# Copying half of a masked weight into natural rows from SyncE's queue instead of ScalarE's, around the last weight piece

## The chip, the core and the metric

The kernel runs on one core of a Trainium2 chip. The metric is device time in microseconds (us) of one execution, taken as the median of several runs. TensorE is written PE in the profile, VectorE DVE, ScalarE ACT, GpSimd POOL and SyncE SP. A name with a q (SPq, ACTq) is the engine's own queue of instructions, from which transfers (DMAs) are issued.

## What is computed

A weight `w` of 1024 x 1024 is pruned: in each group of four consecutive rows k, column by column, the two entries of largest magnitude are kept and the others set to zero. Then 8192 tokens `x` (16 x 512) are multiplied by it and a bias is added. All inputs and the output are bf16.

```python
wg = w.reshape(G, M, D)                       # G = 256, M = 4
mag = jnp.abs(wg)
order = jnp.argsort(mag, 1)
thr = jnp.take_along_axis(mag, order[:, M - N:M - N + 1, :], 1)   # N = 2
mask = mag >= thr
wp = (wg * mask).reshape(D, D)
return jnp.einsum("bsd,df->bsf", x, wp) + b
```

## The kernel before

**The data.** Tokens are worked on in 64 tiles of 128. The 1024 output columns are two halves of 512 (h = 0, 1), one PSUM bank each; there are eight banks, taken in turn. The contraction over k is eight blocks of 128 rows, and the first four (g = 0) and last four (g = 1) are handled apart at the start.

**The weight.** It is loaded into four tiles `w_gh[(g, h)]` of 128 partitions x 4 x 512, with groups on the partitions: partition p holds rows 4p to 4p+3 of its half of k. So the magnitudes of a group lie on one partition, and VectorE finds the mask by maxima and minima (`prep_piece`, lines 126 to 143; line 143 is the multiply that masks). This is done in seven pieces, 0 to 6 in the list at line 61; the last, piece 6, is the whole of g = 1, h = 1. `abs_piece` (112 to 124) makes the magnitudes, on VectorE for pieces 0 and 1 and on ScalarE for the others.

**Natural rows.** In `w_gh` the row order is not that of a block of 128 consecutive rows. `unpack(g, h, c0, c1, eng)` (148 to 150) copies a masked part into `wp_nat[h]`, 128 partitions x 8 x 512, in natural row order: four transfers from SBUF to SBUF, each from 32 partitions x 4 rows into 128 partitions. Over 512 columns one transfer is 128 KB, over 256 columns 64 KB. A `wp_nat` block of g = 1 is needed by the early tiles' second half of k; those of g = 0 are first needed by the main loop.

**The first ten tiles** (T = 10) start before the weight is ready. Half their k (g = 0) is transposed on PE (`transpose_half`, line 160) and copied by ScalarE (line 165), with matching row order, so it multiplies `w_gh` directly (`mm_part`, line 179). ScalarE parks these sums in fp32 (`to_stage`, line 193). The other half (g = 1) comes transposed by one DMA into `xg1` (line 98) and multiplies `wp_nat`, line 179 again. VectorE adds the two halves (`add_stage`, line 197). Their bias is added later (`add_bias`, line 201) into one of four `o_sb` buffers and stored by ScalarE's queue (line 210).

**The main loop** (291 to 313) handles tiles 10 to 62 with all eight blocks of k: 16 matmuls of 128 x 512 per tile at line 301, on two banks. VectorE empties the banks and adds the bias (line 207); while the first ten tiles' results remain, it also does three or four of `add_bias` per tile, ahead of that tile's two emptyings. ScalarE's queue stores (line 313). The last tile is `last_tile` (280 to 289), with its matmuls at line 276 and its last store on SP's queue.

**Transposed tokens** come by DMA transposes on SP's queue (`issue_batch`, line 219): tiles 10-11, then 12-15 (both `xTs`), then eight tiles at a time into two buffers `xTb`.

**The order of the start** is written out by hand in `FRONT` (231 to 241) and kept as the program order. Of its tokens, `P.i` masks piece i; `M.i.t` and `N.i.t.m` multiply piece i for tile t; `X.q.t` multiplies a whole quarter q = 2g + h; `V.h.t` parks and `O.h.t` adds; `U.g.h.c0.c1` unpacks on SP's queue; `Z.g.h.c0.c1` unpacks on ScalarE's; `L.i` issues transpose batch i. On SP's queue the tokens give, before the change: four transfers of `U.1.0.0.256`, four of `U.1.0.256.512`, four of `U.1.1.0.512` (piece 6), then `L.0`, `L.1`, `L.2`. ScalarE's queue has `Z.0.0.0.512` and `Z.0.1.0.512`, eight transfers, after its last `V`. PE's first use of piece 6 is `M.6.0`, eight tiles of which, with `X.3.8` and `X.3.9`, stand between it and the main loop.

**Semaphores of transfers.** There are eight, given to the transfers in turn; a transfer waits until the one that had its semaphore before has landed.

Of the kernel before, what the change touches and what calls it, by code (L numbers as in the profile page):

```python
# [10 lines left out]
def kernel(  # L11
# [7 lines left out]
    nc = tc.nc  # L19
    P = 128  # L20
# [5 lines left out]
    K = tc.keep_in_program_order  # L26
# [36 lines left out]
    w_gh = {(g, h): const.tile([P, 4, FH], bf16, name=f"w_{g}_{h}") for g in range(2) for h in range(2)}  # L63
# [43 lines left out]
    def warm(n):  # L107
        K(nc.tensor.matmul(bank[7][:, :n], lhsT=zeros[:, :P], rhs=zeros[:, :n], start=True, stop=True))  # L108
# [3 lines left out]
    def abs_piece(i, on_act):  # L112
        g, c0, c1 = pieces[i]
        n = c1 - c0
        if n <= 256:
            mag = mags_pool.tile([P, 4, n], bf16, name="mag")[:]
        else:
            mag = const.tile([P, 4, n], bf16, name=f"mag_{i}")[:]
        if on_act:
            K(nc.scalar.activation(mag, w_of(i), Act.Abs))  # L120
        else:
            K(nc.vector.tensor_single_scalar(
                mag.bitcast(u16), w_of(i).bitcast(u16), 0x7FFF, op=Alu.bitwise_and))
        mags[i] = mag

    def prep_piece(i):
        g, c0, c1 = pieces[i]
        n = c1 - c0
        mag = mags.pop(i)
        magv = mag.rearrange("p (a j) f -> p a j f", j=2)  # L130
        hi = tmp.tile([P, 2, FH], bf16, name="hi")[:, :, :n]
        lo = tmp.tile([P, 2, FH], bf16, name="lo")[:, :, :n]
        K(nc.vector.tensor_tensor(hi, magv[:, :, 0, :], magv[:, :, 1, :], op=Alu.max))  # L133
        K(nc.vector.tensor_tensor(lo, magv[:, :, 0, :], magv[:, :, 1, :], op=Alu.min))  # L134
        t1 = tmp.tile([P, FH], bf16, name="t1")[:, :n]
        t2 = tmp.tile([P, FH], bf16, name="t2")[:, :n]
        K(nc.vector.tensor_tensor(t1, hi[:, 0, :], hi[:, 1, :], op=Alu.min))
        K(nc.vector.tensor_tensor(t2, lo[:, 0, :], lo[:, 1, :], op=Alu.max))
        thr = tmp.tile([P, FH], bf16, name="thr")[:, :n]
        K(nc.vector.tensor_tensor(thr, t1, t2, op=Alu.max))  # L140
        mask = tmp.tile([P, 4, FH], bf16, name="mask")[:, :, :n]
        K(nc.vector.tensor_tensor(mask, mag, thr[:, None, :].to_broadcast([P, 4, n]), op=Alu.is_ge))  # L142
        K(nc.vector.tensor_tensor(w_of(i), w_of(i), mask, op=Alu.mult))  # L143

    wp_nat = [const.tile([P, KT, FH], bf16, name=f"wp_nat{h}") for h in range(2)]


    def unpack(g, h, c0, c1, eng=nc.sync):
        for j in range(4):
            K(eng.dma_start(wp_nat[h][:, 4 * g + j, c0:c1], w_gh[(g, h)][32 * j:32 * (j + 1), :, c0:c1]))  # L150

    xT = {}
    own = {}
# [1 line left out]
    def transpose_half(t):  # L155
        own[(0, t)] = next_bank()
        xv = xh[t].rearrange("p (q m) -> p m q", m=4)
        dst = bank[own[(0, t)]][:].bitcast(bf16)[:, :4 * P].rearrange("p (m q) -> p m q", m=4)
        for m in range(4):
            K(nc.tensor.transpose(dst[:, m, :], xv[:, m, :], ident[:]))  # L160

    def copy_half(t):
        xt = const.tile([P, 4, P], bf16, name=f"xT_{t}")
        src = bank[own[(0, t)]][:].bitcast(bf16)[:, :4 * P].rearrange("p (m q) -> p m q", m=4)
        K(nc.scalar.copy(xt[:], src))  # L165
        xT[t] = xt


    def mm_part(q, t, c0, c1, ms=range(4)):
        g, h = divmod(q, 2)  # L170
        if c0 == 0 and q > 0 and 0 in ms:
            own[(q, t)] = next_bank()
        dst = bank[own[(q, t)]][:, c0:c1]
        for m in ms:
            if g == 0:
                lhs, rhs = xT[t][:, m, :], w_gh[(0, h)][:, m, c0:c1]
            else:
                lhs, rhs = xg1[:, m, t * P:(t + 1) * P], wp_nat[h][:, 4 + m, c0:c1]
            K(nc.tensor.matmul(dst, lhsT=lhs, rhs=rhs, start=c0 == 0 and m == 0, stop=c1 == FH and m == 3))  # L179
# [11 lines left out]
    def to_stage(h, t):  # L191
        stage[(h, t)] = const.tile([P, FH], fp32, name=f"stage{h}_{t}")
        K(nc.scalar.copy(stage[(h, t)][:], bank[own[(h, t)]][:]))  # L193

    def add_stage(h, t):
        st = stage[(h, t)][:]
        K(nc.vector.tensor_tensor(st, bank[own[(2 + h, t)]][:], st, op=Alu.add))  # L197

    def add_bias(h, t):
        f = slice(h * FH, (h + 1) * FH)  # L200
        K(nc.vector.tensor_tensor(get_o(t)[:, f], stage.pop((h, t))[:], bias_sb[:, f], op=Alu.add))  # L201
        if (1 - h, t) not in stage:
            store(t)
# [10 lines left out]
    def issue_batch(t0, nb):  # L214
        if nb < 8:
            xt = const.tile([P, KT, nb * P], bf16, name=f"xTs{t0}")
        else:
            xt = xtb.tile([P, KT, nb * P], bf16, name="xTb")
        K(nc.sync.dma_start_transpose(out=xt[:], in_=xf[t0 * P:(t0 + nb) * P, :]))
        for j in range(nb):  # L220
            xN[t0 + j] = xt[:, :, j * P:(j + 1) * P]
# [10 lines left out]
        A.0 P.0 W W W W W W W W w w T.0 T.1 C.0 T.2 T.3 C.1 w T.4 T.5 C.2 w M.0.0 A.1 C.3 M.0.1 P.1 C.4 T.6 T.7 C.5  # L232
        M.0.2 M.0.3 C.6 M.0.4 A.2 M.0.5 M.0.6 C.7 P.2 M.1.0 A.3 M.0.7 M.1.1 A.4 M.1.2 M.1.3 V.0.0 M.1.4 M.1.5 V.0.1
        P.3 M.1.6 V.0.2 M.1.7 V.0.3 T.8 T.9 M.2.0 C.8 M.2.1 C.9 X.0.8 V.0.4 P.4 U.1.0.0.256 X.0.9 V.0.5 V.0.6 M.2.2
        A.5 M.2.3 M.2.4 M.3.0 V.0.7 M.3.1 P.5 U.1.0.256.512 V.0.8 M.2.5 V.0.9 M.2.6 M.3.2 V.1.0 M.2.7 A.6 M.3.3
        M.3.4 M.3.5 M.3.6 V.1.1 P.6 U.1.1.0.512 L.0 L.1 L.2 M.3.7 V.1.2 X.1.8 V.1.3 X.1.9 V.1.4 M.4.0 V.1.5 M.4.1
        V.1.6 M.4.2 V.1.7 M.4.3 M.4.4 V.1.8 M.4.5 V.1.9 Z.0.0.0.512 Z.0.1.0.512 M.4.6 N.5.0.0 M.4.7 N.5.0.1 N.5.0.2
        N.5.0.3 M.5.1 O.0.0 M.5.2 O.0.1 M.5.3 M.5.4 O.0.2 M.5.5 M.5.6 O.0.3 M.5.7 O.0.4 X.2.8 O.0.5 X.2.9 O.0.6
        M.6.0 O.0.7 M.6.1 O.0.8 O.0.9 M.6.2 O.1.0 M.6.3 O.1.1 M.6.4 O.1.2 M.6.5 O.1.3 O.1.4 M.6.6 O.1.5 M.6.7 O.1.6
        X.3.8 O.1.7 X.3.9 O.1.8 O.1.9  # L240
# [1 line left out]
    for tok in FRONT.split():  # L242
        k, *n = tok.split(".")
        n = [int(c) for c in n]
        if k in "MN":
            g, c0, c1 = pieces[n[0]]
            h = c0 // FH
            mm_part(2 * g + h, n[1], c0 - h * FH, c1 - h * FH, n[2:] or range(4))
        elif k in "Ww":
            warm(FH if k == "W" else P)  # L250
        elif k == "A":
            abs_piece(n[0], n[0] >= 2)
        elif k == "P":
            prep_piece(n[0])
        elif k == "T":
            transpose_half(n[0])
        elif k == "C":
            copy_half(n[0])
        elif k == "X":
            mm_part(n[0], n[1], 0, FH)  # L260
        elif k == "V":
            to_stage(*n)
        elif k == "O":
            add_stage(*n)
        elif k == "B":
            add_bias(*n)
        elif k in "UZ":
            unpack(*n, nc.sync if k == "U" else nc.scalar)
        elif k == "L":
            issue_batch(*batches[n[0]])  # L270
    later = [(h, t) for t in range(T) for h in range(2) if (h, t) in stage]
# [19 lines left out]
    for bi, (t0, nb) in enumerate(batches):  # L291
        if bi >= 1 and bi + 2 < len(batches):
            issue_batch(*batches[bi + 2])
        for t in range(t0, t0 + nb):
# [11 lines left out]
            j = (t - T) % 2  # L306
# [35 lines left out]
```

## Time and profile before

| what | us |
|---|---|
| median of three runs | 235.5 (235.1, 235.5, 237.09) |
| the profiled execution | 235.45 |
| its span | 233.7 |
| first matmul of the main loop | 44.2 |
| last `V` copy on ScalarE ends | 26.55 |
| the eight `Z` issues on ScalarE's queue | 25.63 to 34.42 |
| the twelve `U` issues on SP's queue | 19.09 to 30.18, with gaps |
| `L.0`, `L.1`, `L.2` issued on SP's queue | 30.22, 36.09, 41.50 |

The profiled execution is one run with the hardware profiler; the span is from its first to its last recorded instruction, and times in the views count from the start of the span. In lists of waits the columns are the sum in us, how often, and the longest. In lists of groups and of time, "x8" is the number of instructions and the text in brackets is the idle time ahead of the group with what ended it. In DMA lists the last number is us from issue to landing, the median where there are several. The DMA share is the mean busy share of the core's 16 DMA engines as recorded by their packets, and it can exceed 1.

### The profile page before, as it was taken

The numbers are of one execution on the slowest core, as the hardware profiler recorded it, in microseconds if no ns is written. First come the engines' busy times: TensorE is split into PE (matmuls) and PEld (weight loads), VectorE is DVE, ScalarE is ACT, GpSimd is POOL, SyncE is SP. The second block draws the span as 40 slices with busy tenths as digits, with TensorE's granted clock in tenths as the row PEclk, the third lists the DMA queues.
The fourth block names the chain that finished last, engine by engine and source line by source line (L and its number), as shares of the span: only waits on it lengthen the run. The fifth ranks groups of instructions, "written<-read, shape, count | busy, mean of one in ns | idle before, by whom it ended". The sixth has DMA issues, their size and how long they took to land.

```text
span 233.7 us, 2841 instructions
## 1 busy us (share of the span) xinstructions
PE 228.4 (98%) x1188; PEld 114.8 (49%) x1188; DVE 117.5 (50%) x202; ACT 22.0 (9%) x37; POOL 0.7 (0%) x6
## 2 busy tenths in 40 slices
PE   7999998999999999999999999999999999999995
PEld 3978763444444444444444444444444444444443
DVE  4999697897495343244244234334324424423434
ACT  2999500000000000000000000000000000000000
POOL 1000000000000000000000000000000000000000
PEclk9999999999999999999999999999999999999999
DMA  6995499999999202999229922499528950122222
GB/s 197 350 231 126 89 170 222 264 310 205 257 179 380 96 35 90 233 173 204 110 38 253 252 90 90 91 193 174 174 90 178 257 193 20 72 90 93 90 90 90
DMA packets 76700, 38.19 MB, mean 163 GB/s; under 512 B 61840, under 2 KB 68496, under 8 KB 76688
## 3 DMA queue, kind: packets, MB, share of 16 engines
q1 hardware_dynamic: 66192, 19.86, 46.6%
q10 hardware_dynamic: 10496, 18.16, 23.3%
q8 instruction: 9, 0.15, 0.2%
q14 instruction: 3, 0.02, 0.0%
HBM read 3.67 MB, written 16.78 MB: 88 GB/s over the span
## 4 chain that ended last, share of the span: by engine, by line
PE 89%; ACT 3%; DMA 3%; DVE 2%; SPq 1%; issue 0%
PE bank L301 78%; PE bank L179 6%; DMA wp_nat<-w 3%; PE bank L108 2%; PE bank L276 2%; ACT stage L193 1%; PE bank L160 1%; ACT mag L120 1%; SPq L150 1%; DVE w L143 1%; DVE mask L142 1%; ACT xT L165 0%; DVE hi L133 0%; DVE lo L134 0%; DVE thr L140 0%
## 5 line engine op out<-in xcount | busy, mean ns | idle before, releaser
L301 PE MATMUL bank<-wp_nat,xTb 128*128 128x512 bf16 x752 | 162.5, 379 | 0.0
L207 DVE TENSOR_TENSOR o_pair<-bank,bias_sb 128x512 bf16<-128x512 f32 x106 | 68.3, 686 | 98.5 <-PE bank L301 98.4
L301 PEld LDWEIGHTS <-xTb 128*128 128x128 bf16 x752 | 73.6, 98 | 88.7
L301 PE MATMUL bank<-wp_nat,xTs 128*128 128x512 bf16 x96 | 20.9, 379 | 0.0
L179 PE MATMUL bank<-wp_nat,xg 128*128 128x256 bf16 (+1 forms) x112 | 17.7, 318 | 1.3 <-DMA wp_nat<-w 1.3
L179 PE MATMUL bank<-w,xT 128*128 128x256 bf16 (+1 forms) x144 | 17.9, 284 | 0.0
L197 DVE TENSOR_TENSOR stage<-bank,stage 128x512 f32<-128x512 f32 x20 | 13.1, 687 | 4.9 <-PE bank L179 4.9
L179 PEld LDWEIGHTS <-xT 128*128 128x128 bf16 x144 | 14.0, 98 | 3.1
L201 DVE TENSOR_TENSOR o_sb<-stage,bias_sb 128x512 bf16<-128x512 f32 x20 | 12.8, 685 | 4.8 <-DMA out_dram<-o_sb 4.8
L301 PEld LDWEIGHTS <-xTs 128*128 128x128 bf16 x96 | 9.4, 98 | 11.3
L179 PEld LDWEIGHTS <-xg 128*128 128x128 bf16 x112 | 10.9, 98 | 7.9 <-issue 1.6
L193 ACT COPY stage<-bank 128x512 f32<-128x512 f32 x20 | 10.3, 671 | 0.0
L120 ACT ACTIVATE mag<-w 128x1024 bf16<-128x1024 bf16 (+1 forms) x5 | 6.2, 1253 | 0.1
L142 DVE TENSOR_TENSOR mask<-mag,thr 128x1024 bf16<-128x1024 bf16 (+1 forms) x7 | 5.4, 768 | 0.2
L143 DVE TENSOR_TENSOR w<-w,mask 128x1024 bf16<-128x1024 bf16 (+1 forms) x7 | 5.4, 768 | 0.2
L165 ACT COPY xT<-bank 128x512 bf16<-128x512 bf16 x10 | 5.2, 608 | 2.7 <-PE bank L160 2.7
L108 PE MATMUL bank<-zeros 128*128 128x512 bf16 (+1 forms) x12 | 4.2, 509 | 1.2 <-DVE zeros L101 1.2
L276 PE MATMUL bank<-wp_nat,xTb 128*128 128x128 bf16 (+2 forms) x32 | 3.7, 272 | 0.0
L133 DVE TENSOR_TENSOR hi<-mag 128x512 bf16<-128x512 bf16 (+1 forms) x7 | 3.2, 460 | 0.3 <-ACT mag L120 0.3
L160 PE MATMUL bank<-ident,xh 128*128 128x128 bf16 x40 | 3.4, 246 | 0.0
L160 PEld LDWEIGHTS <-xh 128*128 128x128 bf16 x40 | 3.1, 124 | 0.3 <-DMA xh<-in_x_dram 0.3
L108 PEld LDWEIGHTS <-zeros 128*128 128x128 bf16 x12 | 1.5, 135 | 3.4 <-issue 2.2
(16 smaller groups left out, 17.4 us busy)
## 6 DMA issues: line engine op xcount, KB each, us to landing
out_dram<-o_pair ACTq DMA_DIRECT2D x26, 512.0 KB, 3.3
out_dram<-o_sb ACTq DMA_DIRECT2D x10, 256.0 KB, 6.5
w<-in_w_dram SPq DMA_DIRECT2D x3, 512.0 KB, 6.6
xh<-in_x_dram SPq DMA_DIRECT2D x4, 256.0 KB, 4.6
wp_nat<-w ACTq DMA_DIRECT2D x8, 128.0 KB, 6.3
wp_nat<-w SPq DMA_DIRECT2D x8, 64.0 KB, 2.1
wp_nat<-w SPq DMA_DIRECT2D x4, 128.0 KB, 3.9
xh<-in_x_dram ACTq DMA_DIRECT2D x1, 256.0 KB, 4.2
```

Source lines behind the costliest of these rows:

```text
L108: K(nc.tensor.matmul(bank[7][:, :n], lhsT=zeros[:, :P], rhs=zeros[:, :n], start=True, stop=True))
L120: K(nc.scalar.activation(mag, w_of(i), Act.Abs))
L142: K(nc.vector.tensor_tensor(mask, mag, thr[:, None, :].to_broadcast([P, 4, n]), op=Alu.is_ge))
L143: K(nc.vector.tensor_tensor(w_of(i), w_of(i), mask, op=Alu.mult))
L160: K(nc.tensor.transpose(dst[:, m, :], xv[:, m, :], ident[:]))
L179: K(nc.tensor.matmul(dst, lhsT=lhs, rhs=rhs, start=c0 == 0 and m == 0, stop=c1 == FH and m == 3))
L193: K(nc.scalar.copy(stage[(h, t)][:], bank[own[(h, t)]][:]))
L197: K(nc.vector.tensor_tensor(st, bank[own[(2 + h, t)]][:], st, op=Alu.add))
L201: K(nc.vector.tensor_tensor(get_o(t)[:, f], stage.pop((h, t))[:], bias_sb[:, f], op=Alu.add))
L207: K(nc.vector.tensor_tensor(o_sb[:, f], bank[bk][:], bias_sb[:, f], op=Alu.add))
L276: K(nc.tensor.matmul(bank[bk][:, :c1 - c0], lhsT=xN[t][:, kt, :], rhs=wp_nat[h][:, kt, c0:c1], start=kt == 0, stop=kt == KT - 1))
L301: K(nc.tensor.matmul(bank[bks[h]][:], lhsT=xN[t][:, kt, :], rhs=wp_nat[h][:, kt, :], start=kt == 0, stop=kt == KT - 1))
```

## The change

The eight transfers that copy g = 0 into natural rows go from ScalarE's queue to SP's. Those of h = 0 are issued ahead of piece 6's four, those of h = 1 behind them and ahead of `L.0`. The argument `eng` of `unpack` and the token `Z` disappear. The instructions of PE, VectorE and GpSimd and their order are the same; the transfers take other semaphores of the eight.

```diff
-    def unpack(g, h, c0, c1, eng=nc.sync):
+    def unpack(g, h, c0, c1):
         for j in range(4):
-            K(eng.dma_start(wp_nat[h][:, 4 * g + j, c0:c1], w_gh[(g, h)][32 * j:32 * (j + 1), :, c0:c1]))
+            K(nc.sync.dma_start(wp_nat[h][:, 4 * g + j, c0:c1], w_gh[(g, h)][32 * j:32 * (j + 1), :, c0:c1]))
...
-        A.5 M.2.3 M.2.4 M.3.0 V.0.7 M.3.1 P.5 U.1.0.256.512 V.0.8 M.2.5 V.0.9 M.2.6 M.3.2 V.1.0 M.2.7 A.6 M.3.3
-        M.3.4 M.3.5 M.3.6 V.1.1 P.6 U.1.1.0.512 L.0 L.1 L.2 M.3.7 V.1.2 X.1.8 V.1.3 X.1.9 V.1.4 M.4.0 V.1.5 M.4.1
-        V.1.6 M.4.2 V.1.7 M.4.3 M.4.4 V.1.8 M.4.5 V.1.9 Z.0.0.0.512 Z.0.1.0.512 M.4.6 N.5.0.0 M.4.7 N.5.0.1 N.5.0.2
+        A.5 M.2.3 M.2.4 M.3.0 V.0.7 M.3.1 P.5 U.1.0.256.512 U.0.0.0.512 V.0.8 M.2.5 V.0.9 M.2.6 M.3.2 V.1.0 M.2.7
+        A.6 M.3.3 M.3.4 M.3.5 M.3.6 V.1.1 P.6 U.1.1.0.512 U.0.1.0.512 L.0 L.1 L.2 M.3.7 V.1.2 X.1.8 V.1.3 X.1.9
+        V.1.4 M.4.0 V.1.5 M.4.1 V.1.6 M.4.2 V.1.7 M.4.3 M.4.4 V.1.8 M.4.5 V.1.9 M.4.6 N.5.0.0 M.4.7 N.5.0.1 N.5.0.2
...
-        elif k in "UZ":
-            unpack(*n, nc.sync if k == "U" else nc.scalar)
+        elif k == "U":
+            unpack(*n)
```

## The prediction

> **What bounds the kernel now.** I read the engines' shares first, then the waits, then the chain in order of time, and last the single transfers around the one wait that counts.
>
> From the head of the page and the list of waits:
>
> ```profile
> span 233.7 us, 2841 instructions
> PE 228.4 (98%) x1188; PEld 114.8 (49%) x1188; DVE 117.5 (50%) x202; ACT 22.0 (9%) x37; POOL 0.7 (0%) x6
> ...
> PE bank L179 <- DMA wp_nat<-w: 1.3, 1, 1.3
> ```
>
> TensorE has work for 228.4 of 233.7 us. Outside the start and the tail its one wait of weight is 1.3 us, for a transfer into wp_nat. The chain and the stretches around it:
>
> ```profile
> 27.15 0.54 SPq L150
> ...
> 27.73 0.60 SPq L150
> ...
> 28.38 0.95 SPq L150
> ...
> 29.38 6.78 DMA wp_nat<-w
> ...
> 36.20 8.15 PE bank L179 x37
> 44.34 183.03 PE bank L301 x848
> ```
>
> ```profile
> 24.43:27.15 2.72, 2.72 (x23) 1.99 (x21) 2.62 (x3) 2.12 (x5) 0.00 (x0) 1.00 0.29 63
> 27.15:30.22 3.07, 3.07 (x31) 2.74 (x29) 0.65 (x2) 0.00 (x0) 0.00 (x0) 1.00 0.72 133
> 30.22:34.90 4.68, 4.67 (x33) 2.99 (x31) 4.68 (x9) 0.00 (x0) 0.00 (x0) 1.00 1.11 172
> 34.90:36.20 1.30, 0.00 (x1) 0.00 (x1) 0.82 (x2) 0.00 (x0) 0.00 (x0) 1.00 0.56 70
> ```
>
> In the stretches the first columns are length and PE busy; the last three are the granted clock, the DMA share and GB/s. PE is full until 34.90, stands still to 36.20, and is full again until the tail; the clock is 1.00. I call the four transfers of the last weight piece c0 to c3. SP issues c3 at 29.38 and it lands 6.78 us later, at 36.16: that is the wait. Everything behind it is 848 matmuls in 183.03 us, 3.45 us per token tile of 16.
>
> Next, single transfers, from the DMA view cut to their issue times: c0; ScalarE's first; the pair in flight at 30.1 (ScalarE's fourth, then c3); and the transposes of tokens for tiles 10-11 (L0) and 12-15 (L1).
>
> ```profile
> wp_nat<-w SPq DMA_DIRECT2D x1, 128.0 KB, 2.7
> ```
>
> ```profile
> wp_nat<-w ACTq DMA_DIRECT2D x1, 128.0 KB, 3.1
> ```
>
> ```profile
> wp_nat<-w ACTq DMA_DIRECT2D x1, 128.0 KB, 6.9
> wp_nat<-w SPq DMA_DIRECT2D x1, 128.0 KB, 6.8
> ```
>
> ```profile
> xTs<-in_x_dram SPq DMA_TRANSPOSE x1, 10.0
> ```
>
> ```profile
> xTs<-in_x_dram SPq DMA_TRANSPOSE x1, 7.9
> ```
>
> The last column is us from issue to landing. The same 128 KB takes 2.7 to 3.1 with few others in flight and 6.8 to 6.9 in the crowd of ScalarE's eight, c2, c3 and L0.
>
> **The change part by part.** The work on PE, DVE and POOL is the same instructions in the same order; only ScalarE and SP change.
>
> *ScalarE loses eight issues* (25.63 to 34.42, 8.8 us). Its last copy out of PSUM ends at 26.55 and its next work, a store, is issued at 46.31, so nothing stood behind them. Worth 0 by itself. The cover is 12 us of idle ScalarE; without it, up to 8.8 us would come free, but nobody would be there to use them.
>
> *Four issues go ahead of c0.* SP ends its earlier eight at 24.43 and then stands until VectorE's last multiply, which lets c0 go at 27.15:
>
> ```profile
> SPq L150 <- DVE w L143: 2.9, 2, 2.6
> ```
>
> Four issues at the 0.60 of those just before (23.82) and of c1 take 2.4 us, 24.43 to 26.83, inside the 2.7 us hole. They copy the piece masked long before, so no new wait on VectorE stands in front of c0. Each takes over a semaphore that a transfer eight places earlier used, and waits for that one: the first's was issued at 19.09 and took 2.1, so 21.2, past. Cost 0. Without the hole, c0 to c3 would go 2.4 later.
>
> *c0 to c3* are issued from 27.15 at 0.54 to 0.60, as c0 and c1 were; I take it that c2's 0.95 and c3's 0.80 came from ScalarE issuing beside them. c3 then goes at 27.15 + 3 x 0.60 = 28.95. Its flight lies between 2.7 (c0) and 6.8 (c3 before). I take 3.1, the first of ScalarE's, because L0 and ScalarE's stream are both gone from around it and only four earlier 128 KB transfers are near: landing 32.05, 2.85 before PE asks at 34.90. At 6.8 it lands at 35.75, and 0.85 of the wait stays. So this term is -1.30, with ends -1.30 and -0.45.
>
> The rule that speaks against the change is in the Trainium skill, "DMA: Bandwidth & Descriptors", section "Issuing engines are not separate DMA queues": transfers started by different engines share the same 16 DMA engines, so another queue saves only issue time. Taken strictly: before, c0 to c3 and ScalarE's first four were all down by 36.16, 10.53 us after the first issue at 25.63; the same eight from 24.43 would be down at 34.96, 0.06 after PE asks, and the sum would be 234.21. The gain would then come from the hole, not from the queue. The rise from 2.7 to 6.8 with both queues loaded agrees with sharing, but L0 behind c3 also could have made it.
>
> *Four issues go between c3 and L0.* Each waits for the first four's landing (the last at 26.23 + 3.1 = 29.3), past when it is issued. They run 29.55 to 31.95, and are first needed by the first full tile at 42.9 (44.2 less 1.3): at 31.35 + 3.1 = 34.5, or at 6.8, 38.2, they are hidden.
>
> *L0 and all behind it on SP* move from 30.22 to 31.95, 1.7 later. L0 took 10.0 among ScalarE's eight, L1 7.9 almost alone though twice as large. L0 lands between 31.95 + 7.9 = 39.9 and + 10.0 = 42.0, both before 42.9: cost 0, thin at the upper end. L1 is issued at 36.09 + 1.7 = 37.8 and lands at 45.7, wanted at 42.9 + 2 x 3.45 = 49.8. The first transpose of eight tiles took 13.3; issued at 43.2 it lands at 56.5, wanted at 42.9 + 6 x 3.45 = 63.6. The second took 19.3 from 49.40; at 51.1 it lands at 70.4, wanted at 91. The final 64 KB store on SP waits for the last sum on VectorE, not for the queue.
>
> *What is late next*, with PE 1.3 earlier? VectorE ends its tenth addition at 35.73 and then needs 0.69 each against 0.86 per tile of PE, so it catches up within four. Later it waits twice for buffers still being stored:
>
> ```profile
> 54.48 1.29 DVE L201 TENSOR_TENSOR o_sb<-stage,bias_sb 128x512 bf16<-128x512 f32 x2 [1.52 <-DMA out_dram<-o_sb]
> ...
> 63.86 1.29 DVE L201 TENSOR_TENSOR o_sb<-stage,bias_sb 128x512 bf16<-128x512 f32 x2 [3.29 <-DMA out_dram<-o_sb]
> 65.08 1.28 DVE L207 TENSOR_TENSOR o_pair<-bank,bias_sb 128x512 bf16<-128x512 f32 x2
> ```
>
> The last row empties tile 14's banks by 66.36. Four pairs of banks go round, so PE needs them for tile 18 at 44.34 + 8 x 3.45 = 71.9: 5.6 us of room. With PE 1.3 earlier and stores 1.7 later behind the transposes, 3.0 of it goes. Cost 0.
>
> **Sum.** The profiled execution took 235.45, 1.8 outside its span of 233.7; the median of the runs is 235.5, so the two agree. 235.45 - 1.30 = 234.15, a gain of 0.55%. There is no more idle time in PE's middle to win.
>
> **The rivals.**
>
> *The wait stays in part.* If what makes c3 slow is the transfers queued right behind it on SP (L0 before, four copies now), it again takes 6.8, lands at 35.75, and the sum is 235.45 - 0.45 = 235.0; if it does not even start earlier, 235.45. For it: c0, with nothing close behind, took 2.7. Against: c1 and c2, each with another right behind, took at most 3.9 (the same view, at their times), which from 28.95 is 32.85 and early enough. The Trainium skill's section "Queues, rings and completion order" of the same page speaks against it too: an engine takes one ring's transfers in order and alternates only between rings. That c2 beat c3 agrees with it, though it doesn't settle it.
>
> *Slower: SP becomes the bound and L0 comes late.* Place: the first matmul of L301. If all twelve issues cost the worst on SP, 0.95, they run from 24.43 to 35.83; c3 is issued at 31.08, and L0, at 10.0, lands at 45.8. PE then starts L301 at 45.8 instead of 44.2, by L0 or by a c3 that takes 6.8 (37.9 + 8.0 = 45.9): 235.45 + 1.65 = 237.1. With issues at 0.60 and L0 as slow as the 12.7 of xg1's transpose it lands at 44.65: 235.9. It decides once L0 lands after 42.9, and is slower than before once it lands after 44.2. For it: SP's issues did reach 0.95. Against: only while ScalarE issued too, which stops here.
>
> *Slower: the banks.* If the later stores keep VectorE back by more than the 5.6 us of room, PE waits at tile 18 for the rest. Twice the two waits shown (4.8 more), with 1.3 from the earlier PE, would be 6.1: PE waits 0.5, and the sum is 234.65. Only a delay above 6 us would undo the gain.
>
> **How the numbers follow.** The forecast has 0.74. The wait staying in part or whole has 0.11 (235.0 to 235.45). L0 late has 0.10 (235.9 to 237.1, and beyond), the banks 0.05 (234.65 and up). The likeliest one's own range is 233.5 to 234.8: two of the three runs of before lie 0.4 apart, the third 1.6 higher. For 8 in 10 I take 233.5 to 235.9, which holds the forecast, the wait that stays, and L0's nearer case. About 1% is what a measurement of this kernel can tell from no change: below 233.1 nothing in the sum leads, except the scatter (0.06); above 237.8 lead only L0 beyond its bound, or banks with a long stall (0.11); between them 0.83.
>
> **What would show it.** In the profile after, PE's wait at L179 for wp_nat is gone or below 0.2; four more SP issues stand between 24.4 and 27.1; c0 still goes near 27.15; c3 lands by 33 in about 3 us; L301 starts near 42.9; L0 lands before that. A wait of L301 on xTs means the queue's rival is right, a c3 of over 6 us the first, a PE wait on DVE near 68 to 71 us the banks. I am wrong if L0 takes over 11 us behind the copies, or if c0's issue slips past 29.

## The result, and the profile after

The changed kernel took 234.11 us (median of 14 runs, 233.93 to 234.8), the kernel before 235.32 beside it (14 runs, 234.29 to 237.09): a ratio of 0.9949, 95% interval 0.9928 to 0.997. The forecast was 234.15. The ratios leave out runs more than 1.5% above the fastest of their kernel. The profiled execution of the changed kernel took 234.53, its span 232.7 us; its first transfer into wp_nat was issued at 19.70, against 19.09 before, so all that follows starts about 0.5 later.

The head of its page, and the rows of its list of waits on TensorE and on stores:

```profile
span 232.7 us, 2819 instructions
PE 226.9 (97%) x1168; PEld 114.1 (49%) x1188; DVE 117.2 (50%) x202; ACT 22.0 (9%) x37; POOL 0.7 (0%) x6
...
DVE o_sb L201 <- DMA out_dram<-o_sb: 4.5, 2, 3.3
...
PE bank L179 <- ACT xT L165: 0.4, 1, 0.4
```

TensorE's row for wp_nat is gone. Apart from the 1.2 us ahead of its first matmul, which before has too, what is left on it is a 0.4 us wait early on, for an operand that ScalarE copies, and 0.2 for a first load. (20 matmul records are missing from this trace, so busy PE isn't to be compared by its sum.) The chain in order of time, and the stretch in which PE stood still before:

```profile
33.34 10.09 PE bank L179 x46
43.43 1.73 PE bank L301 x8
```

```profile
34.90:36.20 1.30, 1.30 (x8) 0.59 (x7) 1.30 (x4) 0.00 (x0) 0.00 (x0) 1.00 0.85 153
```

PE runs through from line 179 to 301. SP's queue in order of time (start, us): the first and last of the four copies now ahead of c0, then c0, c3, the last of the four copies behind it, L0 and L1.

```profile
25.08 0.60 SPq L150 DMA_DIRECT2D wp_nat<-w  x1
...
27.02 0.61 SPq L150 DMA_DIRECT2D wp_nat<-w  x1
27.72 1.24 SPq L150 DMA_DIRECT2D wp_nat<-w  x1
...
30.30 0.61 SPq L150 DMA_DIRECT2D wp_nat<-w  x1
...
32.95 0.61 SPq L150 DMA_DIRECT2D wp_nat<-w  x1
33.60 1.88 SPq L219 DMA_TRANSPOSE xTs<-in_x_dram  x1
35.53 5.08 SPq L219 DMA_TRANSPOSE xTs<-in_x_dram  x1
```

From the DMA view at their times, c3 and L0, last column us to landing:

```profile
wp_nat<-w SPq DMA_DIRECT2D x1, 128.0 KB, 2.6
```

```profile
xTs<-in_x_dram SPq DMA_TRANSPOSE x1, 5.0
```

c3 lands at 32.9 instead of 36.16, and L0 at 38.6 instead of 40.2, though it was issued 3.4 later. Further on, the two waits of VectorE for stores have hardly moved:

```profile
53.26 1.29 DVE L201 TENSOR_TENSOR o_sb<-stage,bias_sb 128x512 bf16<-128x512 f32 x2 [1.22 <-DMA out_dram<-o_sb]
...
62.61 1.29 DVE L201 TENSOR_TENSOR o_sb<-stage,bias_sb 128x512 bf16<-128x512 f32 x2 [3.26 <-DMA out_dram<-o_sb]
```

### The profile page after: what moved, and what is told of

Read it like the earlier page. It is cut to its first block, busy times and chain, and to the rows that moved or that the text cites. A ratio compares the mean times of both kernels' runs of the same rounds, so it can differ in the third digit from the quotient of the medians.

```text
span 232.7 us, 2819 instructions
## 1 busy us (share of the span) xinstructions
PE 226.9 (97%) x1168; PEld 114.1 (49%) x1188; DVE 117.2 (50%) x202; ACT 22.0 (9%) x37; POOL 0.7 (0%) x6
## 4 chain that ended last, share of the span: by engine, by line
PE 93%; DMA 3%; SPq 1%; ACT 1%; issue 1%; DVE 0%
PE bank L301 78%; PE bank L179 13%; DMA w<-in_w_dram 3%; PE bank L276 2%; SPq L79 1%; ACT xT L165 1%; SPq L71 0%; ACT mag L120 0%; DVE o_sb L286 0%; PE bank L160 0%
## 5 line engine op out<-in xcount | busy, mean ns | idle before, releaser
L301 PEld LDWEIGHTS <-xTb 128*128 128x128 bf16 x752 | 73.6, 98 | 88.8
L193 ACT COPY stage<-bank 128x512 f32<-128x512 f32 x20 | 10.3, 671 | 0.0
L160 PE MATMUL bank<-ident,xh 128*128 128x128 bf16 x40 | 2.9, 221 | 0.4 <-DMA xh<-in_x_dram 0.2
L134 DVE TENSOR_TENSOR lo<-mag 128x512 bf16<-128x512 bf16 (+1 forms) x7 | 3.2, 455 | 0.0
L276 PEld LDWEIGHTS <-xTb 128*128 128x128 bf16 x32 | 2.5, 98 | 1.3
```

The costliest lines, as they stand in the source:

```text
L276: K(nc.tensor.matmul(bank[bk][:, :c1 - c0], lhsT=xN[t][:, kt, :], rhs=wp_nat[h][:, kt, c0:c1], start=kt == 0, stop=kt == KT - 1))
L301: K(nc.tensor.matmul(bank[bks[h]][:], lhsT=xN[t][:, kt, :], rhs=wp_nat[h][:, kt, :], start=kt == 0, stop=kt == KT - 1))
```

## The experiments

Each was run beside the kernel before on the same chip. There were three groups, each on another chip, with medians of before of 235.49, 235.36 and 234.88. Within a group too before scatters (234.07 to 238.43 in the first), and that turned out to be part of the answer. The changed kernel itself was not run again in these groups, so a comparison with its 234.11 may be across chips. Where a kernel adds a helper, line 179 appears as 188, 219 as 228 and 301 as 312. In the extra copies, a destination is an output buffer that isn't used until later; nobody reads them.

Theory A was that ScalarE's transfers in flight beside c3 make it slow; theory B, that the transpose right behind it on SP does.

### One half of the change, and the other

```diff
-    ... U.1.0.256.512 V.0.8 ... Z.0.0.0.512 Z.0.1.0.512
+    ... U.1.0.256.512 U.0.0.0.512 V.0.8 ... Z.0.1.0.512
```

> One half of the change alone: the copies of g = 0, h = 0 go ahead of c0 on SP, those of h = 1 stay on ScalarE's queue, and L0 stands right behind c3. Theory A (ScalarE's transfers in flight beside them make c3 slow): four of them instead of eight, c3 takes 4 to 5 us from about 29, lands by 34, PE's wait is gone, 234.1. Theory B (the transpose right behind c3 on SP makes it slow): c3 takes 6.8 as before, lands at 35.8 to 36.2, 0.85 to 1.3 us of the wait stay, 235.0 to 235.4.

Measured: 234.28 (12 runs, 234.06 to 235.15), ratio 0.9964, interval 0.9938 to 0.999. c3 was issued at 31.12 and took 3.5, with L0 right behind; ScalarE's last copy landed at 33.1, and PE did not wait for c3. Against B.

```diff
-    ... U.1.1.0.512 L.0 ... Z.0.0.0.512 Z.0.1.0.512
+    ... U.1.1.0.512 U.0.1.0.512 L.0 ... Z.0.0.0.512
```

> The other half alone: the copies of g = 0, h = 1 go behind c3 on SP, ahead of L0; those of h = 0 stay on ScalarE's queue. Theory A: four of ScalarE's transfers beside c0 to c3, c3 takes 4 to 5 us, lands by 34, 234.1. Theory B: c3 has copies behind it, not L0, takes about 3, lands by 33, 234.1. If c3 still takes over 6 and the time is 235, then half of ScalarE's stream is enough to make it late and A holds in a stronger form.

Measured: 234.35 (12 runs, 234.02 to 234.53), ratio 0.996, interval 0.9935 to 0.9986. c3, issued at 29.48, took 4.8 and landed at 34.3, 0.5 ahead of PE. No transpose was behind it, only copies; half of ScalarE's stream was enough to take it from 2.7 to 4.8.

So either half alone gives the whole gain: the 1.3 us could be taken away twice.

### L0 right behind c3, without ScalarE's stream

```diff
-    ... U.1.1.0.512 U.0.1.0.512 L.0 L.1 L.2
+    ... U.1.1.0.512 L.0 U.0.1.0.512 L.1 L.2
```

> The changed kernel with L0 moved to stand right behind c3, the copies of g = 0, h = 1 behind L0, and nothing on ScalarE's queue. Theory A: c3 takes about 3 us as in the changed kernel, no wait at line 179, 234.1; the four copies behind L0 land before 43. Theory B: c3 takes 6 to 7, lands near 36 to 37, PE waits 1 us or more, 235 or above.

Measured: 234.2 (12 runs, 234.01 to 235.32), ratio 0.9963, interval 0.9935 to 0.9991. From its DMA view, c3:

```profile
wp_nat<-w SPq DMA_DIRECT2D x1, 128.0 KB, 2.9
```

It was issued at 29.87 and L0 at 30.52, as close behind as before. B falls: a transpose behind c3 on its own queue does not make it slow by itself.

### ScalarE's stream put back beside the changed order

```diff
+    def extra(h, eng):
+        d = dummy()        # an output buffer, viewed as 4 x 512
+        for j in range(4):
+            K(eng.dma_start(d[:, j, :], w_gh[(0, h)][32 * j:32 * (j + 1), :, :]))
...
-    ... V.1.9 M.4.6
+    ... V.1.9 Z.0 Z.1 M.4.6        # Z.h: extra(h, nc.scalar)
```

> The changed kernel plus eight copies of 128 KB on ScalarE's queue from where the kernel before issued its own, into output buffers not yet in use (extra work, read by nobody). c3 has copies behind it, not L0. Theory A: c3 takes 5 to 7 us again, lands at 34 to 36.5, up to 1.3 us of wait come back, 234.3 to 235.4; L0's issue goes from 1.9 back to 4 to 6. Theory B: c3 stays near 3, no wait, 234.1.

Measured: 234.39 (12 runs, 234.18 to 235.32), ratio 0.9961, interval 0.9934 to 0.9988. c3, issued at 30.92, took 4.1, landed at 35.0, and a piece of the wait is back. From its DMA view, and its list of waits:

```profile
wp_nat<-w SPq DMA_DIRECT2D x1, 128.0 KB, 4.1
...
PE bank L188 <- DMA wp_nat<-w: 0.2, 1, 0.2
```

A in its direction, but weaker than forecast: 4.1, not 5 to 7. c3 was issued 0.6 later than in the changed kernel and flew 1.4 longer, and PE came to it at 34.8 instead of 35.3, so the slack of 2.3 that the changed kernel has was gone. The time hardly moved: the stream alone, put back, does not bring back the 1.2 us.

### ScalarE's stream kept, L0 taken away from behind c3

```diff
-    ... U.1.1.0.512 L.0            # the kernel before
+    ... U.1.1.0.512 D.0 L.0        # D.0: four extra copies on SP
```

> The kernel before, its eight copies on ScalarE's queue kept, with four extra copies of 128 KB (into an output buffer not yet in use) on SP between c3 and L0. So ScalarE's stream is whole, and only the transpose is taken away from behind c3. If ScalarE's stream alone makes c3 slow (theory A), it takes 6 to 7 us, lands near 36, and the time stays at 235.0 to 235.5. If it takes both the stream and L0 right behind c3 (theory C), c3 takes 4 to 5, lands at 33.5 to 35, and the time is 234.1 to 234.4.

Measured: 234.74 (12 runs), ratio 0.9979, interval 0.9947 to 1.0011. The profiled execution, of 234.27, has c3 at 4.8, down at 34.2, and no wait. That is theory C's figure, but five of the twelve runs lie between 235.56 and 237.22. Inconclusive: the times alone don't tell a late c3 from a late L0, which here was issued at 35.04.

### Both suspects together again

```diff
-    ... U.1.1.0.512 U.0.1.0.512 L.0 L.1 L.2 ... V.1.9 M.4.6       # the changed kernel
+    ... U.1.1.0.512 L.0 U.0.1.0.512 L.1 L.2 ... V.1.9 Z.0 Z.1 M.4.6
```

> The changed kernel with L0 right behind c3 (the copies of g = 0, h = 1 behind L0) and, as extra work, eight copies on ScalarE's queue into output buffers not yet in use. This puts both suspects back together while the four copies ahead of c0 stay on SP. Theory C (both together): c3 takes 5.5 to 8 us from about 30.3, lands at 36 to 38, PE waits 1 to 3 us, 235.3 to 237. Theory A (stream alone, 4 to 4.5 us as seen with copies behind c3): lands near 34.9, 234.2 to 234.6.

Measured: 236.5 (12 runs, 235.0 to 240.4), ratio 1.0041, interval 1.0005 to 1.0077. The same transfers with L0 behind the four copies took 234.39, on another chip. Its list of waits:

```profile
PE bank L312 <- DMA xTb<-in_x_dram: 0.9, 1, 0.9
...
PE bank L188 <- DMA wp_nat<-w: 0.4, 1, 0.4
```

c3 took 4.6, so C's 5.5 to 8 was not met in this profile. The time fell into C's range in part for another reason: the first transpose of eight tiles came late. L1's issue waited 2.0 for L0 to land, because in this order L1 takes over L0's semaphore; the kernel before has no such wait. So this run does not price the two suspects alone. Between these two profiles, stream and transpose take longer where L0 is close behind c3: L0 took 8.3 here against 4.95 with the copies ahead of it, and ScalarE's last two copies 6.9 and 6.7 against 4.3 and 3.75.

### The kernel before, twice more

> The kernel before, once more, for a second profile: its runs spread from 234.07 to 238.4 while those of every kernel without the wait stay within 234.0 to 235.3. If c3's lateness is what varies, the wait at line 179 equals the run's time outside the profile's fixed part less 234.1: another length than 1.3 us, and the rest of the trace alike.

> The kernel before, a third profile, for the same purpose: the wait of PE for c3 and c3's flight differ from the 1.3 and 6.8 us of the first profile, and the time of the profiled execution follows the wait one for one.

Measured: 234.13 and 235.57. In the first, c3 is issued at 29.20 and the same row reads

```profile
wp_nat<-w SPq DMA_DIRECT2D x1, 128.0 KB, 4.8
```

so it is down at 34.0, before PE asks, and there is no wait at line 179. In the second it took 6.7, close to the 6.8 of the first profile and not another length as expected, and the list of waits has

```profile
PE bank L179 <- DMA wp_nat<-w: 1.3, 1, 1.3
```

Taking the wait off each: 235.45 - 1.30 = 234.15, 235.57 - 1.3 = 234.3, 234.13 - 0 = 234.13. In these three the time follows the wait one for one, and the wait comes and goes from one execution to the next. They show only 0 and 1.3; that the runs without a profile, from 233.96 up, have values between and above is likely but not shown.

### Where the copies stand on SP's queue

All eight behind c3:

```diff
-    ... U.1.0.256.512 U.0.0.0.512 V.0.8 ... U.1.1.0.512 U.0.1.0.512 L.0
+    ... U.1.0.256.512 V.0.8 ... U.1.1.0.512 U.0.0.0.512 U.0.1.0.512 L.0
```

> The changed kernel with all eight copies of g = 0 behind c3 and none ahead of c0, so the hole on SP ahead of c0 stays empty. If the gain comes from taking ScalarE's stream away from beside c3: c3 is issued near 29, takes under 3.5 us, no wait at line 179; L0 is issued near 34.8, takes about 5 and lands near 40, still ahead of its use; 234.1. If the gain came only from the hole (eight transfers take 10.5 us from the first issue, whichever queue): c3 down near 37.7, a wait of 2.8, 236.9.

Measured: 234.26 (12 runs, 233.96 to 234.86), ratio 0.9981, interval 0.9963 to 1.0. c3 was issued at 29.02; L0 was issued at 34.88 and took 4.4, down at 39.3. From its DMA view, c3:

```profile
wp_nat<-w SPq DMA_DIRECT2D x1, 128.0 KB, 2.7
```

The hole on SP was not needed. Eight copies on c3's own queue, close behind, leave it alone, where eight on the other queue cost it 1.4 to 4 us.

All eight ahead of c0:

```diff
-    ... U.0.0.0.512 V.0.8 ... U.1.1.0.512 U.0.1.0.512 L.0
+    ... U.0.0.0.512 U.0.1.0.512 V.0.8 ... U.1.1.0.512 L.0
```

> The changed kernel with all eight copies of g = 0 ahead of c0 and L0 right behind c3. Eight issues at 0.65 from 24.4 overrun the hole: c0 goes at 29.6, c3 at 31.6 and lands at 34.2 if it takes 2.6, 0.7 ahead of PE: no wait, 234.1. If c3 takes over 3.3, or the issues cost more than 0.70, up to 0.5 us of wait come: 234.6.

Measured: 234.83 (12 runs, 234.32 to 235.49), ratio 0.9998, interval 0.9975 to 1.0022. Here c0 was issued at 30.53, 0.9 later than worked out (about 0.5 of it because this execution's first loads came later), c3 at 32.42, and it landed at 35.3, just as PE came to it. PE did not stand still for it in this profile. The slack ahead of c0 is real, but eight issues use it up. On the same chip the kernel takes 0.57 us more than the one with all eight behind; that c3 comes too late in other executions would explain it, but is not shown.

### Two doses

Sixteen transfers ahead of c0 (the last kernel with eight extra copies):

```diff
-    ... U.0.0.0.512 U.0.1.0.512 V.0.8
+    ... U.0.0.0.512 U.0.1.0.512 D.0 D.1 V.0.8
```

> As the last, with eight more copies of 128 KB on SP ahead of c0 (into output buffers not yet in use, extra work). Sixteen issues at 0.65 from 24.4 put c0 at 34.8, c3 at 36.8, down at 39.4: PE waits 4.5 us at line 179, L0 lands at 42.4 ahead of its use, 234.1 + 4.5 = 238.6. If SP's issues are not what sets c0's time, the time stays below 236.

Measured: 241.25 (4 runs, 240.61 to 242.26), ratio 1.028, interval 1.0239 to 1.032. c0 went at 35.55 and c3 at 37.45, down at 40.35; the waits came as forecast, but the time is 2.7 above. Waits, and stretches by time (length, PE busy; third from the end the granted clock):

```profile
PE bank L188 <- DMA wp_nat<-w: 4.3, 3, 3.7
```

```profile
35.50:36.50 1.00, 0.00 (x0) 0.00 (x0) 0.38 (x1) 0.00 (x0) 0.00 (x0) 1.00 0.86 208
36.50:37.50 1.00, 0.00 (x0) 0.00 (x0) 0.00 (x0) 0.00 (x0) 0.00 (x0) 0.77 0.81 201
37.50:38.10 0.60, 0.00 (x0) 0.00 (x0) 0.00 (x0) 0.00 (x0) 0.00 (x0) 0.50 0.82 190
...
40.40:42.00 1.60, 1.60 (x4) 0.54 (x4) 0.69 (x1) 0.00 (x0) 0.00 (x0) 0.50 1.15 261
42.00:44.00 2.00, 2.00 (x6) 0.73 (x5) 0.69 (x1) 0.00 (x0) 0.00 (x0) 0.53 1.20 244
44.00:47.00 3.00, 3.00 (x15) 1.37 (x14) 2.26 (x4) 0.00 (x0) 0.00 (x0) 1.00 1.09 227
```

PE stops at 34.4; from about 37 its granted clock is 0.50, and it stays so until nearly 44, well after the matmuls have begun again. From 38.1 that is some 5.8 us, of which 0.6 are waits: 5.2 at half speed lose 2.6. 234.1 + 4.3 + 2.6 = 241.0.

Sixteen extra copies between the last four and L0:

```diff
-    ... U.0.1.0.512 L.0
+    ... U.0.1.0.512 D.0 D.1 D.0 D.1 L.0
```

> The changed kernel with sixteen more copies of 128 KB on SP between the last four and L0 (into output buffers not yet in use, extra work). c3 is as in the changed kernel. Sixteen issues at 0.65 put L0 at 42.5; at 5 us it lands at 47.5, 4.6 after the main loop could start: 238.7, with the wait at line 301's counterpart for xTs and none at line 179. If L0 were slack-free only at its old place, or lateness were absorbed later, less than 2 us come.

Measured: 243.57 (4 runs, 240.53 to 245.8), ratio 1.0331, interval 1.0268 to 1.0394. The profile is of the longest run: L0 was issued at 44.15 and took 7.5, down at 51.65, and the wait stands where the rival had put it.

```profile
PE bank L312 <- DMA xTs<-in_x_dram: 8.7, 1, 8.7
```

PE stops at 43.0, and the granted clock was 0.50 from 46.8 to 57.0; PE had work again from 51.7, so 5.3 us at half speed lose 2.65, and 234.1 + 8.7 + 2.65 = 245.45. The direction and the place are those of the rival; the size is not, because L0 was slower than 5 (ScalarE had begun to issue stores beside it) and the clock fell. That the stores slowed it is not shown.

## Why the prediction was right, step by step

**What bounds it, and the sum.** Right: PE's one wait was the whole of what could be won. -1.30 was forecast, and the medians differ by 235.32 - 234.11 = 1.21. That they agree so closely is partly luck: the term came from one execution of a kernel whose wait is 0 in one profile and 1.3 in two. The gain is the middle of a scattering wait that the change takes away, and much of it is in the spread: 14 runs lie within 0.9 us, where before had 2.8. The forecast treated 6.8 us as c3's flight; it is one value of a scattering flight, and this is what the prediction did not see.

**ScalarE's eight issues, worth 0.** Right; no chain passes through them, before or after.

**Four issues ahead of c0, cost 0.** Right. They ran from 25.08 to 27.63 at 0.65 apiece, and c0 followed VectorE's multiply (26.45 and 1.22, ending at 27.67) by 0.05. The hole is not what brought the gain: with nothing ahead of c0 the time is about the same (234.26), and with eight ahead c3 lands just as PE comes to it.

**c0 to c3.** Flight 2.6 where 3.1 was taken, landing at 32.9 where 32.05 was forecast, the issue being 1.35 later (VectorE ended 0.54 later in this execution, c0's own issue took 1.24). The slack of 2.85 covered it.

**The rule that speaks against the change.** The Trainium skill's "DMA: Bandwidth & Descriptors", section "Issuing engines are not separate DMA queues", read strictly, gave 236.9 for the kernel with all eight copies behind c3; it took 234.26, with c3 at 2.7. That the engines are shared agrees with these traces (c3 took 2.6 to 3.4 without the other queue, 4.1 to 6.8 beside four or more of its copies). That a queue is worth only its issue time does not: eight copies behind c3 on its own queue left it at 2.7. The Trainium skill's section "Queues, rings and completion order" of the same page gives the order that would do this: in order within a ring, in turn between rings. The profiles without ScalarE's stream agree, with c3 at 2.6 to 2.9 in five of them and 3.4 in the sixth, whatever stands behind it. But being alone is not enough to be fast: in the changed kernel the copies issued just ahead of c0, from 25.72 to 27.02, took 3.5 to 4.1 with nothing on ScalarE's queue.

**L0 and all behind it.** The forecast was too dark, which cost it nothing: L0 was issued at 33.60, later than the 31.95 forecast, but took 5.0, not 7.9 to 10.0, and its issue 1.88 in place of 5.82, so that L1 and the first transpose of eight tiles went 0.6 and 0.85 earlier than before instead of 1.7 later. The step that failed is "move from 30.22 to 31.95, 1.7 later", carried over to all behind it: I took SP's time for a transpose as fixed, and it was shorter in every profile in which ScalarE's copies were gone.

**What is late next.** Nothing, as forecast: the banks' room was not touched, since the stores' waits stayed at 1.22 and 3.26.

**The rivals.** "The wait stays in part" falls with the kernel that has L0 right behind c3: 2.9. "L0 comes late" is real in its place, but L0 landed at 38.6 and the main loop started at 43.4, so it needs some 5 us more on SP than the change adds. "The banks" never came up.

**What stays open.** ScalarE's stream takes c3 from about 2.7 to between 4.1 and 4.8, and to 3.5 where only the last of its four copies were still landing. What adds two more in two profiles of before out of three isn't settled: L0 alone does not do it, both together did not in the one profile of that kernel, and the order with copies in L0's place scattered too. The longest runs of before in the first group (four of 35 between 237.65 and 238.43) have mean granted clocks of 0.992 to 0.993, where the two doses have 0.979 to 0.993; a wait long enough for the clock to fall is a guess that nothing here tests, as none of them was profiled. Nor is it known why one issue near 27 us takes 0.89 to 1.96 in most kernels, with ScalarE's stream and without, where 0.60 is the rule, or why the copies issued just before it take up to 4.1.

## What to carry to other kernels

When a small transfer is on the critical path, look at which others are in flight beside it on the other queue: putting them behind it on the same queue let it finish in 2.6 to 3.4 us instead of 4.8 to 6.8, at 0.65 us of issue time for each. Before sizing such a wait, profile the kernel more than once or look at the spread of its runs, because a wait for a crowded transfer scatters. And keep a standstill of TensorE short: 1.3 us cost 1.3, but 4.3 cost about 7.

## What the runs showed of the hardware that was not expected

**A transpose's issue takes longer while the other queue's copies are in flight.** L0's issue on SP took 1.88 to 2.13 us in the seven profiles in which none of ScalarE's copies was in flight any more. It took 2.66 to 3.69 in the four in which a part of them was, and 3.95, 5.46 and 5.82 beside the whole stream, in the three profiles of before. Its landing went from 4.4 to 5.3 in the first group (7.5 in the kernel whose L0 met the stores) to 9.4 to 10.3 in the last.

**The clock falls after a standstill and returns late.** With PE idle from 34.4 the granted clock was 1.00 until 37.0, then 0.50 for 6.83 us; with PE idle from 43.0 it was 1.00 until 46.8, then 0.50 for 10.24 us. It returned 5.7 and 5.3 us after the matmuls had begun again. After the 1.3 us of before it stayed at 1.00. The Trainium skill's "TensorE: Matmul & The Clock Gate", section "Part 1: The HAM clock gate", states that an idle window of about 3.4 us brings half rate, and that the window runs free. The 6.83 and 10.24 us at half rate agree with two and three such windows. The first fall does not agree with a window that is idle as a whole: it came after only 2.6 us without a matmul, and here the measurement decides.
